# One queue for x and B, one ring of PSUM banks and a new order ahead of the first product, in an S5 scan with a GEGLU feed-forward block

## The chip, the cores and the metric

The kernel runs on one core of a Trainium2 chip. The metric is the device time of one execution in microseconds (us). A profile comes with a *span*, from the first to the last instruction; in the runs shown here the time is about 2 us above the span. A run that is over 1.5% above the fastest of its kernel counts as slow; ratios use fast runs alone. Each run also comes with the mean clock that TensorE was granted, as a share of the full one.

Engines: PE is TensorE (PEld its weight loads), DVE is VectorE, ACT is ScalarE, POOL is GpSimd, SP is SyncE, which here only issues transfers. PSUM is the memory that TensorE's products are written to; the pools below hold eight buffers of it, called banks here.

## The reference, cut to what matters

```python
xn = layernorm(x)                                   # x: 1 x 2048 x 512
# A: diagonal state space model, P = 512 complex states
Bu   = xn @ B_bar.T                                 # B_re, B_im
h[t] = Lam_bar * h[t-1] + Bu[t]
s    = 2 * real(h @ C.T) + xn * Dskip
# B: feed-forward, F = 1376
g    = silu((gelu(xn @ w_gate) * (xn @ w_up)) @ w_down)
out  = x + s * g
```

## The kernel before

The 2048 positions are four stages of 512 (`s`). TensorE's order is u(0), then for each stage: eleven steps (`j`) of gate and up, with the four y products of the stage before laid between them; u of the next stage; the four down products f. VectorE turns u into a real scan by rotating it with cos and sin tables (`pp`, `qq`, `Wt`), scans (`Ft`) and rotates back (`hst`), which y reads. ScalarE evicts u, gate and up from PSUM, that is, copies them out, so that their banks come free. Six "table products" on VectorE build the cos and sin tables first. The order of VectorE's instructions comes from a small model in the kernel with two clocks, `clk["pe"]` and `clk["dve"]`.

```python
ps_mm = ctx.enter_context(tc.tile_pool(name="ps_mm", bufs=4, space=bass.MemoryType.PSUM))  # u, gate, up, B transposes
ps_f  = ctx.enter_context(tc.tile_pool(name="ps_f",  bufs=2, space=bass.MemoryType.PSUM))  # down, warm-up
ps_y  = ctx.enter_context(tc.tile_pool(name="ps_y",  bufs=2, space=bass.MemoryType.PSUM))  # y, x transposes
...
for m in range(M):                                   # x, first stage, SyncE's queue
    nc.sync.dma_start(out=x_tok[:, m, :], in_=x_r[:, m, :])
...
for ri, src in enumerate((A_B_re, A_B_im)):          # B, ScalarE's queue
    nc.scalar.dma_start(out=Bn[:, ri, :, :], in_=...)
...                                                  # then all weights, SyncE's queue
dummies(12)                                          # warm-up products
b_transposes(0)
...
b_transposes(1)                                      # B imaginary, ahead of x on TensorE
dummies(4)
...                                                  # layernorm of x, transposes, copies to xnT
ACT(out=sb[:], in_=ang[:], func=AF.Sin, scale=TWO_PI)
ACT(out=cb[:], in_=kr[:], func=AF.Sin, scale=-TWO_PI, bias=halfpi[:])
nc.vector.tensor_copy(out=sh[:], in_=sb[:])          # fp32 to bf16
nc.vector.tensor_copy(out=ch[:], in_=cb[:])
nc.gpsimd.tensor_copy(out=v4(sa[:]), in_=sh[...])    # widening of the table
...
if s == 0:
    ...
else:
    if j == M: ln_small(s + 1)                       # layernorm of the next stage
    if 6 <= j < 6 + M: ln_out(s + 1, j - 6)          # transposed by SyncE into xnT
    if j in (4, 6, 8, 10): epi(s - 1, m, y_mm(...), ...)
```

## Time and profile before

| | before |
|---|---|
| median of three timed runs | 202.88 us (202.27 to 203.77) |
| the run that was profiled | 201.35 us, span 199.2 us, clock 1.00 |
| first u product starts | 15.03 us |
| B's imaginary half lands | 10.41 us |
| last matmul ends | 195.8 us |

The chain that ended last as shares of the span by engine:

```profile
DVE 47%; PE 30%; ACT 13%; DMA 5%; issue 3%; SPq 0%; ACTq 0%; DVEq 0%
```

TensorE is busy for 93% of the span, yet the chain runs for 47% through VectorE. The two don't contradict each other: while TensorE is busy nearly all the time, many of its waits end on VectorE's work, directly or through ScalarE or a transfer that had waited for it, and the chain then follows VectorE back for many microseconds of unbroken work.

### The profile page before, as it was taken

How to read it: one execution, taken by the hardware profiler on the slowest of the kernel's cores; microseconds unless marked ns; L12 is line 12 of the kernel's file. 1: busy time of each engine (PE TensorE's matmuls, PEld its weight loads, DVE VectorE, ACT ScalarE, POOL GpSimd, SP SyncE). 2: the span in 40 equal slices, each digit the busy share in tenths (PEclk: the TensorE clock that was granted, in tenths of full speed). 3: DMA queues.
4: the chain of work that ended last, by engine and by line, in shares of the span. 5: the costliest groups of instructions: out<-in, count | busy, mean ns of one | idle time of the engine just before them, and what ended most of it. 6: DMA issues, size and time to landing. Idle time of an engine off the chain costs nothing.

```text
span 199.2 us, 2595 instructions
## 1 busy us (share of the span) xinstructions
PE 184.6 (93%) x924; PEld 86.7 (43%) x924; DVE 167.9 (84%) x286; ACT 109.2 (55%) x198; POOL 17.8 (9%) x35
## 2 busy tenths in 40 slices
PE   7478799999999999979999999979989999999993
PEld 2243344444444444444444444434434444454452
DVE  4449999989999779999999889999999999832444
ACT  2434988999327975646425995645423644441210
POOL 3406630000000060000000050000000000000000
PEclk9999999999999999999999999999999999999999
DMA  5999955300000002320000002320000000000001
GB/s 160 357 361 354 174 148 170 79 2 3 0 0 0 0 3 53 79 53 26 0 2 3 0 0 54 81 54 26 0 0 0 3 0 26 26 26 30 26 21 60
DMA packets 21164, 12.26 MB, mean 62 GB/s; under 512 B 11456, under 2 KB 21152, under 8 KB 21152
## 3 DMA queue, kind: packets, MB, share of 16 engines
q1 hardware_dynamic: 20064, 11.05, 21.0%
q10 hardware_dynamic: 1088, 1.05, 1.6%
q8 instruction: 7, 0.11, 0.2%
q14 instruction: 5, 0.04, 0.1%
HBM read 7.38 MB, written 2.10 MB: 48 GB/s over the span
## 4 chain that ended last, share of the span: by engine, by line
DVE 47%; PE 30%; ACT 13%; DMA 5%; issue 3%; SPq 0%; ACTq 0%; DVEq 0%
DVE Ft L389 10%; PE f_ps L445 10%; DVE pp L359 6%; PE y_ps L464 6%; DVE qq L359 6%; PE up_ps L430 6%; PE g_ps L425 6%; ACT junk L519 5%; DMA Bn<-in_A_B_im_dram 4%; ACT ub L437 3%; DVE Wt L363 3%; DVE at L438 3%; ACT gt L435 3%; DVE hst L363 3%; DVE yg L482 2%
## 5 line engine op out<-in xcount | busy, mean ns | idle before, releaser
L425 PE MATMUL g_ps<-xnT,wg 128*128 128x512 bf16 (+1 forms) x176 | 45.2, 379 | 0.0
L430 PE MATMUL up_ps<-xnT,wu 128*128 128x512 bf16 (+1 forms) x176 | 45.2, 379 | 0.0
L445 PE MATMUL f_ps<-wd,at 128*128 128x512 bf16 (+1 forms) x176 | 39.5, 379 | 1.2 <-DVE g L452 1.2
L435 ACT ACTIVATE gt<-g_ps 128x512 bf16<-128x512 f32 (+1 forms) x44 | 26.0, 591 | 16.5 <-PE g_ps L425 16.3
L340 PE MATMUL u_ps<-xnT,BT 128*128 128x512 bf16 x128 | 28.7, 379 | 4.9 <-ACT U L345 2.2
L389 DVE TENSOR_TENSOR_SCAN Ft<-rho,it,Wt 128x512 bf16<-128x512 f32 x24 | 30.3, 1276 | 0.0
L437 ACT ACTIVATE ub<-up_ps 128x512 bf16<-128x512 f32 (+1 forms) x44 | 26.2, 595 | 6.6 <-PE up_ps L430 6.6
L464 PE MATMUL y_ps<-C,hst 128*128 128x512 bf16 x120 | 28.7, 379 | 0.4 <-DVE hst L363 0.3
L450 ACT ACTIVATE th<-f_ps 128x512 f32<-128x512 f32 x16 | 9.6, 597 | 34.3 <-PE f_ps L445 34.3
L445 PEld LDWEIGHTS <-at 128*128 128x128 bf16 (+1 forms) x176 | 17.1, 98 | 22.6 <-issue 2.7
L430 PEld LDWEIGHTS <-wu 128*128 128x128 bf16 (+1 forms) x176 | 17.6, 100 | 20.4
L425 PEld LDWEIGHTS <-wg 128*128 128x128 bf16 (+1 forms) x176 | 17.2, 100 | 18.4
L345 ACT ACTIVATE U<-u_ps 128x512 bf16<-128x512 f32 x32 | 18.2, 598 | 11.4 <-PE u_ps L340 11.3
L438 DVE TENSOR_TENSOR at<-gt,ub 128x512 bf16<-128x512 bf16 (+1 forms) x44 | 18.3, 419 | 6.8 <-ACT ub L437 6.6
L340 PEld LDWEIGHTS <-BT 128*128 128x128 bf16 x128 | 12.4, 98 | 20.0 <-issue 6.0
L464 PEld LDWEIGHTS <-hst 128*128 128x128 bf16 x120 | 11.5, 98 | 14.5 <-DVE hst L363 1.4
L452 DVE SCALAR_TENSOR_TENSOR g<-th,f_ps 128x512 f32<-128x512 f32 x16 | 10.8, 678 | 7.6 <-ACT th L450 7.6
L482 DVE TENSOR_TENSOR yg<-y_ps,g 128x512 bf16<-128x512 f32 x15 | 10.2, 683 | 3.2 <-PE y_ps L469 3.1
L363 DVE TENSOR_TENSOR Wt<-pp,qq 128x1024 bf16<-128x1024 bf16 x16 | 10.8, 688 | 0.2
L363 DVE TENSOR_TENSOR hst<-pp,qq 128x1024 bf16<-128x1024 bf16 x16 | 10.5, 687 | 0.1
L519 ACT ACTIVATE junk<-x_tok 128x512 bf16<-128x512 bf16 x16 | 10.0, 628 | 0.3
L359 DVE TENSOR_TENSOR pp<-U,cos_b 128x2048 bf16<-128x2048 bf16 x8 | 9.8, 1222 | 0.1
(106 smaller groups left out, 157.5 us busy)
## 6 DMA issues: line engine op xcount, KB each, us to landing
out_dram<-ot SPq DMA_DIRECT2D x15, 128.0 KB, 1.7
x_tok<-in_A_x_dram SPq DMA_DIRECT2D x3, 512.0 KB, 3.9
wd<-in_B_w_down_dram SPq DMA_DIRECT2D x1, 1280.0 KB, 10.7
x_tok<-in_A_x_dram SPq DMA_DIRECT2D x4, 128.0 KB, 2.2
Bn<-in_A_B_re_dram ACTq DMA_DIRECT2D x1, 512.0 KB
Bn<-in_A_B_im_dram ACTq DMA_DIRECT2D x1, 512.0 KB, 7.2
wg<-in_B_w_gate_dram SPq DMA_DIRECT2D x1, 512.0 KB, 8.8
wu<-in_B_w_up_dram SPq DMA_DIRECT2D x1, 512.0 KB
```

Source lines behind the costliest of these rows:

```text
L340: nc.tensor.matmul(u_ps[:, :], lhsT=BT[:, ri, kt, pt * P : (pt + 1) * P], rhs=xnT[:, kt, cols], start=(kt == 0), stop=(kt == KT - 1),)
L359: TT(out=box[key][:], in0=src()[:], in1=tab[:, hs, :].unsqueeze(1).to_broadcast(W), op=ALU.mult)
L363: return lambda: TT(out=dst()[i], in0=box["pp"][:, i, :, :], in1=box["qq"][:, 1 - i, :, :], op=op)
L389: nc.vector.tensor_tensor_scan(out=box["F"][:, ri, q, :], data0=rho[:, pt : pt + 1].to_broadcast([P, TS]), data1=box["W"][:, ri, q, :], in ...
L425: nc.tensor.matmul(g_ps[:fs, :], lhsT=wg[:, kt, fsl], rhs=xnT[:, kt, cols], start=(kt == 0), stop=(kt == KT - 1))
L430: nc.tensor.matmul(u_ps[:fs, :], lhsT=wu[:, kt, fsl], rhs=xnT[:, kt, cols], start=(kt == 0), stop=(kt == KT - 1))
L435: ACT(out=gt[:fs], in_=g_ps[:fs, :], func=AF.Gelu_apprx_tanh)
L437: ACT(out=ub[:fs], in_=u_ps[:fs, :], func=AF.Copy)
L438: dve(now() + 0.9, 0.34, lambda: TT(out=at[:fs, j, :], in0=gt[:fs], in1=ub[:fs], op=ALU.mult))
L445: nc.tensor.matmul(f_ps[:, :], lhsT=at[:fs, k, m0 : m0 + P], rhs=wd[:fs, k, :], start=(k == 0), stop=(k == NFT - 1))
L464: nc.tensor.matmul(y_ps[:, :], lhsT=hst[:, j // NPT, j % NPT, m0 : m0 + P], rhs=C2[:, j // NPT, j % NPT, :], start=(j == 0), stop=False,)
L519: ACT(out=junk[:], in_=x_tok[:, s * M + m, :], func=f, accum_out=sx[:, s, i, m : m + 1])
```

## The change

The intent is to start the first product earlier and to let TensorE run on without waiting. The diff, cut to its core:

```diff
-    ps_mm = ... bufs=4 ...   ps_f = ... bufs=2 ...   ps_y = ... bufs=2 ...
+    psum = ctx.enter_context(tc.tile_pool(name="psum", bufs=8, space=bass.MemoryType.PSUM))
     (every PSUM tile: tag="ps" of this pool)
-        nc.scalar.dma_start(out=Bn[:, ri, :, :], in_=src...)
+        nc.sync.dma_start(out=Bn[:, ri, :, :], in_=src...)
-    dummies(12); b_transposes(0); (pt) ; b_transposes(1); dummies(4); (statistics) ... (x transposes)
+    dummies(10); (pt) ; dummies(3); (statistics, norms 0 and 1)
+    b_transposes(0)
+    tps = [t_xn0(0, xs[0]), t_xn0(1, xs[1])]
+    xs += [norm0(2), norm0(3)]
+    b_transposes(1)
+    (xnT copies 0, 1) ; tps += [t_xn0(2, xs[2]), t_xn0(3, xs[3])] ; (xnT copies 2, 3)
-    ACT(out=sb[:], ...Sin); ACT(out=cb[:], ...Sin); nc.vector.tensor_copy(sh, sb); nc.vector.tensor_copy(ch, cb)
+    ACT(out=sh[:], ...Sin); ACT(out=ch[:], ...Sin)
+    (four more Sins of 4 columns in fp32 for c1, s1, cS, sS)
+    Y_AT = (5, 7, 9, 10)
-            (nc.sync).dma_start(out=out_td[...])          # last tile, in halves
+            (nc.sync, nc.scalar)[i].dma_start(out=out_td[...])
-    clk["pe"] = 10.3 ; clk["dve"] = 10.3 ; dve(10.3, 2.8, ln1_stats)
+    clk["pe"] = 9.5  ; clk["dve"] = 11.0 ; dve(11.0, 2.8, ln1_stats)
-                    if j == M: ln_small(s + 1)
-                    if 6 <= j < 6 + M: ln_out(s + 1, j - 6)
-                if j in (4, 6, 8, 10): (y)
+                    if j == M - 1: ln_small(s + 1)
+                    if 5 <= j < 5 + M: ln_out(s + 1, j - 5)
+                if j in Y_AT: (y)
```

## The prediction

> **What bounds the kernel now.** I read the page's busy shares first, then the chain of work that ended last, then the timeline of the first 30 us, then TensorE's own waits. From the page of the kernel before:
>
> ```profile
> span 199.2 us, 2595 instructions
> ...
> PE 184.6 (93%) x924; PEld 86.7 (43%) x924; DVE 167.9 (84%) x286; ACT 109.2 (55%) x198; POOL 17.8 (9%) x35
> ...
> PE   7478799999999999979999999979989999999993
> ```
>
> TensorE is the fullest engine. How much of its 184.6 us is needed? Counted in 512-column products after the first real product: 128 for u, 352 for gate and up, 176 for down, 120 for y, 8 for the last y in halves (16 of 256 columns), 16 for the diagonal (64 of 128 columns): 800. The chain of waits has undisturbed stretches such as "153.39 0.86 PE g_ps L425 x4", 0.216 us a product, so they need 800 x 0.2158 = 172.6 us. The first of them starts at 15.03, the last matmul ends at about 195.8, so the stretch lasts 180.8 us: 8.2 us are lost inside it, 15.0 us lie ahead of it, 3.4 us behind it (last VectorE halves and the output transfer). Everything that can be won is in the 15.0 and the 8.2. The chain of waits (start, length, what) names what holds the 15.0:
>
> ```profile
> 1.18 2.05 DMA x_tok<-in_A_x_dram
> 3.25 7.16 DMA Bn<-in_A_B_im_dram
> 10.46 1.07 PE tb_ps L142 x16
> 11.53 0.86 PE w_ps L135 x4
> 12.65 0.76 DVE xnT L203 x2
> ```
>
> So the second half of B, issued at 3.25, lands only at 10.4; TensorE transposes it in its program order ahead of x, whose first two blocks VectorE had normalised by 8.8. The timeline shows what happens just behind:
>
> ```profile
> 15.03 4.48 PE L340 MATMUL u_ps<-xnT,BT 128*128 128x512 bf16 x20 [0.53 <-DVE xnT L207]
> ...
> 16.57 0.46 ACT L228 ACTIVATE cb<-kr,halfpi 128x196 f32<-128x196 f32 x1
> ...
> 16.90 1.89 POOL L242 COPY sa<-sh 128x2048 bf16<-128x2048 bf16 x1 [0.59 <-DVE sh L229]
> 16.93 0.58 ACT L345 ACTIVATE U<-u_ps 128x512 bf16<-128x512 f32 x1
> 17.06 1.84 DVE L230 CAST ch<-cb 128x196 bf16<-128x196 f32 x1 [0.23 <-ACT cb L228]
> ...
> 18.93 1.91 ACT L328 ACTIVATE ca<-ch 128x2048 bf16<-128x2048 bf16 x1 [1.43 <-DVE ch L230]
> ...
> 20.75 3.15 ACT L345 ACTIVATE U<-u_ps 128x512 bf16<-128x512 f32 x6
> ...
> 21.38 2.75 PE L340 MATMUL u_ps<-xnT,BT 128*128 128x512 bf16 x12 [1.87 <-ACT U L345]
> ```
>
> Read it upwards: TensorE stops because its four banks are full; ScalarE stands behind the ca copy, which waits for a VectorE cast that takes 1.84 us where the same cast of sh took 0.26. Last, TensorE's waits inside the 8.2 us:
>
> ```profile
> PE u_ps L340 <- ACT U L345: 2.2, 2, 1.9
> PE u_ps L340 <- DMA xnT<-xn: 2.2, 2, 1.1
> PE f_ps L445 <- DVE g L452: 1.2, 4, 0.4
> ...
> PE y_ps L464 <- DVE hst L363: 0.3, 1, 0.3
> ```
>
> These are 5.9 us by this view. Measured from start to start of the products around each break (a broken stream also refills) the same places cost about 2.6, 2.5, 2.0 and 0.7 us, 7.8 in all.
>
> **What the Trainium skill says.** (1) "SBUF — State Buffer", section "Who interferes with whom": a cast in a two-port mode and a GpSimd instruction lock each other out for the whole instruction. The trace agrees: the 1.84 us cast runs beside the 1.89 us GpSimd copy and ends just after it. The section also says that a VectorE instruction with at most one SBUF input outside those modes doesn't contend; that would hold for the bn_stats, 0.615 us each. No line here has one beside a GpSimd copy. (2) "DMA: Bandwidth & Descriptors", section "Issuing engines are not separate DMA queues": transfers of several issuers interleave on the same 16 engines. The trace agrees: from 5.5 to 9.5 the weights on SyncE's queue and B on ScalarE's queue share about 355 GB/s. (3) "ScalarE: Activation LUTs", section "What ACT_TABLE_LOAD costs": about 0.19 us plus 0.83 ns an element, 0.09 more for a pointer operand. The 196-column Sin with a bias took 0.46, the one without 0.37, which agrees; four Sins of 4 columns come to 0.2 to 0.3 us each.
>
> **The change part by part.**
>
> *One queue.* x's four issues end at 2.6; B's two now follow at once, and the weights only then. x flows from 1.9 at the issue rate (128 KB each 0.46 us), so its 512 KB are over near 4.2. Then 1 MB of B at the full 350 KB/us seen from 6 us on: real part over at 5.7, imaginary at 7.1, landed about 5.9 and 7.4 against 10.4. The weights lose nothing that counts: total bytes are the same, gate and up are first needed after the u products, and the last of x's second block, whose last packets run near 10.9 now, should be in by 11.
>
> *New order.* VectorE: bn, aggregate as before to 5.0; pf waits for the transpose behind ten warm-up products (5.65); third aggregate and eps end at 6.9; two norms to 7.65; thn, a1; two more norms after GpSimd's power, 8.0 to 8.8. TensorE: B real 6.1 to 7.2, two x transposes to 7.95, B imaginary to 9.0, two x transposes to 9.6. VectorE copies xnT four times at 0.38: 8.8 to 9.55 and, after the last transposes, to about 10.3. ScalarE's four BT evictions at 0.97 end at 10.6, and the last two are not needed by the first product. With 0.3 for a slipping GpSimd power, the first product starts near 10.6: 4.4 us earlier.
>
> *Casts removed.* Sin writes bf16 itself, so 0.26 + 1.84 us leave VectorE, and four small Sins (0.9 us) come to ScalarE. From 10.4: angles 1.45, Sins and small Sins to 13.3, U0, ca to 15.8, then seven evictions at 0.52 to 19.4, table load 1.3. TensorE's u products run 10.6 to 17.5.
>
> *Ring of eight.* With eight banks u writes all its eight tiles unstopped; the gate tile at 17.5 takes the bank of u0, evicted at 13.9; the fifth gate tile at 24.4 takes that of the first gate tile, evicted near 21.4. So the 2.0 us stall goes, and the 0.5 us one near 47. The f tiles take banks of long evicted u tiles: their 2.0 us go.
>
> *Layernorm and y one step earlier or later.* The transposes of xn are issued at steps 5 to 8 rather than 6 to 9, 1.73 us earlier. The two waits for them are about 1.1 each: 2.5 us go. y waits one step more for hst, but VectorE comes late there (below): of 0.7 us, 0.5 stays.
>
> *Output on two queues.* The two last issues don't collide now (0.43 us apart from ot to ot): 0 to 0.2.
>
> Sum: 4.4 + 2.6 + 2.0 + 2.5 + 0.2 = 11.7 less 0.5 for new small waits: 11.2 us. Check from below: 10.6 + 172.6 + 1.4 for waits, refills and pacing + 3.4 = 188.0 us of span, 11.2 under 199.2. Taking 11.2 from the 202.88 median: 191.7 us.
>
> **The rivals.** *VectorE becomes the bound.* From 21.5 to 65 it has hardly a gap, so the hst of the first stage come when its work is done. I followed the kernel's own ordering rule with its new clocks (9.5 and 11.0): at0 now stands behind four table products, not five. VectorE would be there at 19.8, ScalarE gives ub0 only at 21.9, so 2 us of the gain are idle on VectorE. Adding its durations from there puts the last hst at 65.1 (70.96 now), TensorE reaches y at 63.4 and needs the first of that pair at 63.9: a wait of about 0.4, which is why 0.5 stays in my sum. If VectorE is 2 us later than I think, y waits for 2 us: 193.7. In later stages VectorE needs about 35.5 us against TensorE's 43, so it catches up.
>
> *B's transfer is hidden anyway.* If VectorE's chain and not B sets the first product, only the order helps. My lists give 10.3 for VectorE and 9.6 for TensorE, so VectorE takes over as the last step, but 4 us earlier. A slip of the power on GpSimd, or x slower beside nothing, makes it 12: 193.
>
> *The ring couples stages.* A bank comes free only in turn, so a slow VectorE reader of f or y could stop gate tiles eight later. g is read within 2 to 3 us, eight tiles are 5 to 7 us: against it. Only with a late VectorE at the y steps would it cost 1 us.
>
> *SyncE's queue.* The transposes of xn for stage 1 stand behind eight C transposes that issue from 15.6 to 27.4 whatever is done, then 1 MB of x. They then land near 35, and TensorE wants them at 36.6: 1.6 us to spare. Failing that costs 1 us.
>
> **Range and chances.** Floor: nothing lost inside, 10.3 + 172.6 + 3.4 = 186.3 of span, 190.0 of time. Two of the rivals together give 194.8. I take 189.8 to 194.6 round 191.7. Even half of the start's gain and half the waits would be 3%, so faster 0.96, same 0.03, slower 0.01.
>
> **What would show it.** Right: the imaginary half of B lands near 7.4; the first u product starts between 10.2 and 11.2; u's 32 products run as one group; no f_ps and no xnT wait above 0.3 us; no 1.84 us cast. Wrong: a first product after 12, VectorE before at0 idle for over 3 us, y_ps waits of over 1 us, gate tiles that wait for y's reader, or xnT waits in stage 1.

## The result, and the profile after

The changed kernel takes 190.52 us (median of 4, 189.84 to 190.78) against 203.32 (median of 4, 202.27 to 204.12). The ratio is 0.9368, 95% interval 0.9315 to 0.9422. Ratios here are the mean time of one kernel's fast runs over that of the other's of the same rounds, so not quite the ratio of the medians. The span of the profiled runs went from 199.2 to 188.8.

Page of the changed kernel: span, busy time, and the chain by engine.

```profile
span 188.8 us, 2587 instructions
...
PE 181.2 (96%) x918; PEld 85.9 (45%) x918; DVE 165.5 (88%) x284; ACT 108.0 (57%) x202; POOL 21.7 (12%) x35
...
PE 89%; ACT 4%; DMA 2%; DVE 2%; SPq 1%; issue 0%
```

The chain is TensorE's own work for 89% now. What is left to VectorE, ScalarE and DMA lies at the start and in one stretch, from 55 to 65 us.

The chain of waits of the changed kernel at the start (start, length, what):

```profile
2.66 4.57 DMA Bn<-in_A_B_re_dram
...
8.80 1.07 PE tb_ps L140 x16
9.87 0.24 PE tp L171 x4
...
10.94 1.24 PE u_ps L333 x5
```

The first product starts at 10.94 instead of 15.03. The chain still begins with the transfer of B: its real half lets TensorE begin at 7.27 and is the longest piece ahead of the first product; the imaginary half lands at 8.76 (issued at 3.13, 5.6 us to landing in the table of transfers), TensorE transposes it from 8.80 on, and only then come the last two blocks of x.

The timeline of the changed kernel behind the first product:

```profile
10.94 7.07 PE L333 MATMUL u_ps<-xnT,BT 128*128 128x512 bf16 x32 [0.62 <-DVE xnT L212]
...
12.31 1.89 POOL L236 COPY sa<-sh 128x2048 bf16<-128x2048 bf16 x1 [3.94 <-ACT sh L219]
12.54 2.47 DVE L151 BATCH_NORM_STATS2 st<-x_tok 128x6 f32<-128x512 bf16 x4 [0.29 <-DMA x_tok<-in_A_x_dram]
...
15.50 3.50 ACT L338 ACTIVATE U<-u_ps 128x512 bf16<-128x512 f32 x7
...
21.43 0.42 DVE L431 TENSOR_TENSOR at<-gt,ub 128x512 bf16<-128x512 bf16 x1 [1.28 <-ACT ub L430]
```

All 32 u products run as one group, although ScalarE evicts seven of the eight tiles only from 15.50 on: eight banks hold them. The four statistics take 2.47 us beside GpSimd's copy and took 2.46 us alone in the kernel before, so they are not held up as the cast was. The last line shows VectorE idle for 1.28 us ahead of the first `at`, waiting for ScalarE.

TensorE's waits of the changed kernel, all of them (total, times, longest):

```profile
PE tb_ps L140 <- DMA Bn<-in_A_B_re_dram: 1.3, 1, 1.3
PE w_ps L133 <- DVE halfpi L109: 1.2, 1, 1.2
PE y_ps L457 <- DVE hst L356: 1.0, 1, 1.0
PE u_ps L333 <- DVE xnT L212: 0.6, 1, 0.6
```

The waits for `U`, for the transposed `xn` and for `g` are gone. One wait behind the first product remains, of y for `hst`, and it has grown from 0.3 to 1.0. The timeline of VectorE just there:

```profile
62.83 0.43 DVE L431 TENSOR_TENSOR at<-gt,ub 128x512 bf16<-128x512 bf16 x1 [0.78 <-ACT ub L430]
63.17 1.22 DVE L352 TENSOR_TENSOR qq<-Ft,sin_b 128x2048 bf16<-128x2048 bf16 x1
64.42 0.69 DVE L356 TENSOR_TENSOR hst<-pp,qq 128x1024 bf16<-128x1024 bf16 x1
```

`hst` stands behind an `at` in VectorE's order, and that `at` waits 0.78 us for ScalarE. TensorE has begun y at 63.62 and can't go on before 65.17. In the chain of waits the stretch before this, from 55.2 to 62.8, is all ScalarE's: its evictions, and between them six squares of the next stage's layernorm (`junk`, 0.63 us each), which make it late. Moving those was not tried.

### The profile page after: what moved, and what is told of

Read it like the earlier page. It is cut to its first block, busy times and chain, and to the rows that moved or that the text cites. A ratio compares the mean times of both kernels' runs of the same rounds, so it can differ in the third digit from the quotient of the medians.

```text
span 188.8 us, 2587 instructions
## 1 busy us (share of the span) xinstructions
PE 181.2 (96%) x918; PEld 85.9 (45%) x918; DVE 165.5 (88%) x284; ACT 108.0 (57%) x202; POOL 21.7 (12%) x35
## 4 chain that ended last, share of the span: by engine, by line
PE 89%; ACT 4%; DMA 2%; DVE 2%; SPq 1%; issue 0%
PE f_ps L438 20%; PE up_ps L423 18%; PE g_ps L418 18%; PE u_ps L333 15%; PE y_ps L457 14%; DMA Bn<-in_A_B_re_dram 2%; ACT junk L512 2%; PE y_ps L462 2%; PE tb_ps L140 1%; ACT ub L430 1%; PE y_ps L490 1%; SPq L89 1%; ACT gt L428 1%; DVE qq L352 1%; DVE xnT L212 0%; DVE hst L356 0%
## 5 line engine op out<-in xcount | busy, mean ns | idle before, releaser
L438 PE MATMUL f_ps<-wd,at 128*128 128x512 bf16 (+1 forms) x176 | 38.7, 379 | 0.0
L338 ACT ACTIVATE U<-u_ps 128x512 bf16<-128x512 f32 x32 | 17.7, 602 | 8.3 <-PE u_ps L333 8.3
L333 PEld LDWEIGHTS <-BT 128*128 128x128 bf16 x128 | 12.4, 98 | 15.1 <-issue 0.7
L457 PEld LDWEIGHTS <-hst 128*128 128x128 bf16 x120 | 11.5, 98 | 15.1 <-DVE hst L356 2.0
L527 ACT ACTIVATE xn<-x_tok,nb,rs 128x512 bf16<-128x512 bf16 x12 | 9.8, 814 | 6.1 <-POOL nb L523 6.1
L475 DVE TENSOR_TENSOR yg<-y_ps,g 128x512 bf16<-128x512 f32 x15 | 10.3, 684 | 1.9 <-PE y_ps L462 1.8
L356 DVE TENSOR_TENSOR hst<-pp,qq 128x1024 bf16<-128x1024 bf16 x16 | 10.6, 689 | 0.2
L517 POOL TENSOR_SCALAR sx<-sx 128x4 f32<-128x4 f32 x2 | 1.4, 684 | 81.2 <-ACT junk L512 81.2
```

Of the source, the lines that this page charges most:

```text
L333: nc.tensor.matmul(u_ps[:, :], lhsT=BT[:, ri, kt, pt * P : (pt + 1) * P], rhs=xnT[:, kt, cols], start=(kt == 0), stop=(kt == KT - 1),)
L338: ACT(out=U[:, ri, q, :], in_=u_ps[:, :], func=AF.Copy)
L356: return lambda: TT(out=dst()[i], in0=box["pp"][:, i, :, :], in1=box["qq"][:, 1 - i, :, :], op=op)
L438: nc.tensor.matmul(f_ps[:, :], lhsT=at[:fs, k, m0 : m0 + P], rhs=wd[:fs, k, :], start=(k == 0), stop=(k == NFT - 1))
L457: nc.tensor.matmul(y_ps[:, :], lhsT=hst[:, j // NPT, j % NPT, m0 : m0 + P], rhs=C2[:, j // NPT, j % NPT, :], start=(j == 0), stop=False,)
```

## The experiments

"The changed kernel" below is the kernel after the change; its ratio to the kernel before is 0.9368. Each ratio is to the kernel before on the same chip in the same rounds. A difference of two ratios times 203.5 us gives the microseconds quoted as "by the ratios". It compares runs of different rounds, partly on different chips; from the two 95% intervals its uncertainty is estimated at 1.3 to 1.5 us where the run had five rounds (the early and late y, the clocks, the layernorm steps and what follows), and at 1.7 to 2.0 us where it had three. Medians and ranges take in slow runs, ratios don't.

### B back in ScalarE's queue

```diff
-        nc.sync.dma_start(out=Bn[:, ri, :, :], ...)
+        nc.scalar.dma_start(out=Bn[:, ri, :, :], ...)
```

> The changed kernel with B back in ScalarE's queue, beside the weights. If the single queue is what brings B in early: the imaginary half lands near 10.4 instead of 8.76, the first u product starts near 13.2 instead of 10.94, the rest is unmoved: span 191.1, time 192.8 us (1.012 of the changed kernel). If the new order of VectorE alone makes the start and B is hidden anyway: first product below 11.5, time within 0.5 us of 190.5.

Measured: 194.51 us (193.03 to 196.31), ratio 0.9501 (0.9417 to 0.9585), 2.7 us worse by the ratios. The three fast runs have spans of 191.0 to 193.2 against the 191.1 expected. The profiled run fell in the slow state (196.31 us), so its length proves nothing, and how much of what it shows the fast runs share stays open. Its chain, and the two stretches around B's landing (length; busy time of PE, PEld, DVE, ACT and POOL with their instructions; PEclk, the granted clock; the DMA share and GB/s):

```profile
3.42 8.95 DMA Bn<-in_A_B_im_dram
12.42 1.89 PE tb_ps L140 x16
```

```profile
8.50:12.40 3.90, 0.00 (x0) 0.00 (x0) 0.33 (x1) 0.84 (x1) 0.00 (x0) 0.82 1.08 365
12.40:17.70 5.30, 4.76 (x29) 3.28 (x30) 2.82 (x8) 2.99 (x7) 0.65 (x1) 0.50 1.10 363
```

On the shared engines B's imaginary half landed at 12.4 here, 2 us later than in the profile of the kernel before. TensorE idled for 4.2 us, its granted clock fell to 0.50, and the transposes took 1.89 us instead of 1.07. The rival, a time within 0.5 us of 190.5, falls by the fast runs alone, the best of which took 193.03: the new order alone does not make the gain.

### The queue alone

```diff
 (in the kernel before)
-        nc.scalar.dma_start(out=Bn[:, ri, :, :], ...)
+        nc.sync.dma_start(out=Bn[:, ri, :, :], ...)
```

> The kernel before with B behind x in SyncE's queue and nothing else. By the theory B's imaginary half lands near 8.8, the first product starts near 13.4 instead of 15.03 and TensorE's later waits stay (about 7.8 us): time 1.6 us under before, 201.5. By the rival that the queue is the main part of the start's gain: first product near 11, 4 us under before.

Measured: 199.86 us (199.01 to 201.87), ratio 0.9801 (0.9719 to 0.9883); whether that is 2% is unclear by the interval. The profile agrees with the theory: B lands near 9.0, the first product starts at 13.60, and all of TensorE's later waits are as before; the span, 197.8, is 1.4 under that of the profile before. The timed gain, about 4 us by the ratios, is the rival's figure, though the first product is not where the rival had it. The difference seems to be the kernel before's own: its timed runs of these rounds had spans of 200.5 to 203.5 and clocks of 0.972 to 0.991, where its profile had 199.2 and 1.00. The last experiment takes this up.

### Three pools again

```diff
-    psum = ... bufs=8
+    ps_mm = ... bufs=4 ; ps_f = ... bufs=2 ; ps_y = ... bufs=2     (tiles as in the kernel before)
```

> The changed kernel with the three PSUM pools of four, two and two banks as before. If the ring removed the waits on ScalarE's U and on VectorE's g: waits of u, g or up tiles of 1 to 3 us in the first 25 us, 0.5 near 45 and about 2 us before f tiles come back, time 193.5 to 195.5. If the earlier VectorE and ScalarE work has made them disappear by itself: under 1 us, time below 191.5.

Measured: 195.09 us (194.43 to 195.68), ratio 0.9552, 3.7 us worse by the ratios. TensorE's waits:

```profile
PE f_ps L440 <- DVE g L447: 2.0, 2, 1.1
...
PE u_ps L335 <- ACT U L340: 1.0, 2, 0.7
```

The waits return, as the theory had it. One part is smaller: the wait of u in the first stage was 1.9 us before and is 0.7 here, where ScalarE, without the wait for the casts, comes to the remaining u tiles 4.56 us behind the first product instead of 5.72. The ring takes that rest too.

### The casts back

```diff
-    ACT(out=sh[:], ...Sin) ; ACT(out=ch[:], ...Sin) ; (four small Sins)
+    ACT(out=sb[:], ...Sin) ; ACT(out=cb[:], ...Sin)
+    nc.vector.tensor_copy(out=sh[:], in_=sb[:]) ; nc.vector.tensor_copy(out=ch[:], in_=cb[:])
```

> The changed kernel with Sin writing fp32 and VectorE casting to bf16 as before, no small Sins. If the cast's lock with GpSimd cost time: a cast of about 1.8 us is back, ca and the U evictions start 1 us later, VectorE's bn_stats 2.1 us later, and the wait of y for hst grows from 1.3 to 2 to 3 us; with eight banks u itself does not stop: time 191 to 192. If VectorE has slack there (it idles 1.3 us before at): the wait of y grows by under 0.5 us, time within 0.5 us of 190.5.

Measured: 191.08 us (190.66 to 191.83), ratio 0.9369: no difference from 0.9368. The timeline of this kernel shows the slow cast back:

```profile
12.49 1.84 DVE L224 CAST ch<-cb 128x196 bf16<-128x196 f32 x1 [0.23 <-ACT cb L222]
...
22.12 0.42 DVE L433 TENSOR_TENSOR at<-gt,ub 128x512 bf16<-128x512 bf16 x1 [0.26 <-ACT ub L432]
```

VectorE loses 2.1 us to the casts but idles only 0.26 us ahead of `at` instead of 1.28; the rest is ScalarE's, which gives `at` its input 1.0 us later, counted from the first product. y's wait stays 0.9. With a ring of eight banks, removing the 1.84 us cast is worth nothing measurable: half of what VectorE saved, it spent waiting.

### y one step earlier, and later

```diff
-    Y_AT = (5, 7, 9, 10)
+    Y_AT = (4, 6, 8, 10)
```

> The changed kernel with y at steps 4, 6, 8, 10 as before. If the step of y sets its wait for hst: the y wait grows from 1.3 to between 2 and 3 us because hst comes at the same time and y asks 1.7 us earlier: span 189.8 to 190.5, time 191.5 to 192.2. If VectorE's order moves with it (hst is pulled ahead of at tiles when y asks): the wait stays below 1.8 us, time within 0.5 of 190.5.

Measured: 193.84 us (192.42 to 194.59), ratio 0.9498, 2.6 us worse. More than expected. The timeline of TensorE, and the stretch just behind the wait (columns as above):

```profile
65.39 2.64 PE L457 MATMUL y_ps<-C,hst 128*128 128x512 bf16 x6 [2.67 <-DVE hst L356]
```

```profile
65.20:69.00 3.80, 3.62 (x12) 1.59 (x13) 1.67 (x4) 0.14 (x1) 2.55 (x6) 0.55 0.00 0
```

The wait is 2.67 us, and behind it the clock is 0.55 for 3.8 us: six products take 2.64 us instead of the 1.68 us that six take in the changed kernel. By the trace's clock records it is 0.50 for 3.41 us, from 65.53 on. Five of the six runs have a mean clock of 0.99, which such a stretch would give (estimated: 1 - 0.5 x 3.41 / 192 = 0.991); one has 0.999 and the shortest span. So a wait of this length can be paid twice, but need not be: in the profile of the kernel before, the wait of 2.50 us for B was followed by the full clock.

```diff
-    Y_AT = (5, 7, 9, 10)
+    Y_AT = (6, 8, 9, 10)
```

> The changed kernel with y at steps 6, 8, 9, 10. If y is merely too early for VectorE: the wait of 1.3 us falls below 0.3, no other appears, span 187.6, time 189.3. If y's readers then hold up the banks of later tiles or hst moves later too: another wait of 1 us, time as 190.5 or above.

Measured: 190.49 us (190.28 to 192.66), ratio 0.9365: no gain. The wait of y is gone and two others are there:

```profile
PE up_ps L423 <- DVE g L445: 1.9, 2, 1.4
...
PE u_ps L333 <- DVE yg L475: 1.0, 1, 1.0
```

An up tile waits for the reader of an f tile, a u tile for the reader of a y tile. In the ring a bank comes free in turn only, so a VectorE reader that is late for f or y stops a product that has nothing to do with it. The changed kernel's profile has no such wait; one step of y is enough to bring them. This profile is of one of the two longer runs, though (spans of 190.1 and 190.7; the other four have 188.2 to 188.6), so most runs may wait less.

### The ordering clocks of before

```diff
-    clk["pe"] = 9.5  ; clk["dve"] = 11.0 ; dve(11.0, 2.8, ln1_stats)
+    clk["pe"] = 10.3 ; clk["dve"] = 10.3 ; dve(10.3, 2.8, ln1_stats)
```

> The changed kernel with the clocks that order VectorE's work set back to 10.3 and 10.3, which puts at0 behind five table products instead of four. If VectorE's 1.28 us of idleness before at0 is what makes hst late for y: the idle time goes below 0.2, hst comes 1.1 us earlier, the y wait falls from 1.3 to below 0.4, span 187.8, time 189.5. If the lost time is made up or lost elsewhere before y: the y wait stays above 1, time 190.5.

Measured: 189.21 us (188.78 to 190.06), ratio 0.9276 (0.9239 to 0.9313), 1.9 us better than the changed kernel by the ratios. All of TensorE's waits:

```profile
PE w_ps L133 <- DVE halfpi L109: 1.2, 1, 1.2
PE u_ps L333 <- DVE xnT L212: 0.6, 1, 0.6
PE tb_ps L140 <- DMA Bn<-in_A_B_re_dram: 0.2, 1, 0.2
```

On VectorE a fifth table product, of 1.25 us from 20.05 on, fills the idle time before the first `at`, and no wait behind the first product is left. The edit moves many instructions of VectorE, so the idle time is not all that it changes; also `hst` no longer stands behind the late `at`. But the wait of y, 1.3 us with its refill, is what the run wins in the profile beside the 0.6 us earlier start of this run; the two make up nearly all of the 2.0 us between the spans, 188.8 and 186.8.

### The layernorm steps of before, alone and with the early y

```diff
-                    if j == M - 1: ... if 5 <= j < 5 + M: ln_out(s + 1, j - 5)
+                    if j == M: ...     if 6 <= j < 6 + M: ln_out(s + 1, j - 6)
```

> The changed kernel with the layernorm steps back at 6 to 9. If the earlier steps removed the two waits for the transposed xn (1.2 and 1.3 us): they come back with 1 us each, time 192.5. If the later y steps 9 and 10 give the transposes room anyway (TensorE has 1.9 us more work behind step 9): no such wait above 0.3 us, time within 0.4 of 190.5; and ScalarE's wait of 4.0 us for GpSimd's nb shrinks.

Measured: 190.56 us (190.29 to 191.15), ratio 0.9341 (0.9302 to 0.9379). No wait for the transposed `xn` comes back. So the earlier layernorm step, to which the prediction gave 2.5 us, is not needed for them. Both old steps together:

> The changed kernel with both the layernorm steps (6 to 9) and the y steps (4, 6, 8, 10) as before. Either alone left no wait for the transposed xn. If each of the two is enough by itself: both undone bring back two waits of about 1.2 us each, on top of the 2.8 us wait of y seen with the early y: time 2.0 to 2.5 us above that run, 196. If it is the ring or the start that removed the xnT waits: none above 0.3 us, time as with the early y alone, 193.8.

Measured: 195.31 us (193.88 to 197.35), ratio 0.9585, against 0.9498 with the early y alone: 1.8 us more. Beside the same wait of y, 2.7, the table of waits has:

```profile
PE u_ps L333 <- DMA xnT<-xn: 1.6, 3, 1.1
```

The waits return when both are undone. Either the earlier layernorm or the later y (two y products behind step 9 rather than one) suffices; the change does the same thing twice.

### x ahead of B's imaginary half on TensorE

In the kernels with the changed start, the first product follows B's landing. Landing of the imaginary half and start of the first product, in us, from eight profiles: 8.76 and 10.94 (the changed kernel), 8.31 and 10.49 (three pools), 8.98 and 11.17 (y early), 7.85 and 10.23 (y late), 8.47 and 10.66 (casts), 8.14 and 10.33 (old clocks), 9.11 and 11.29 (layernorm), 8.25 and 10.43 (both steps). The difference is 2.18 or 2.19 in seven of them, 2.38 where B lands earliest. This does not single out the imaginary half: the first product also starts 3.47 to 3.67 behind the start of TensorE's work on the real half, and in all eight TensorE comes to the imaginary half less than 0.2 us before it can start on it. In the seven, TensorE's wait ahead of that work ends with the real half's landing. In the eighth (y late) no such wait is left, because its warm-up products last until 6.93.

```diff
-    b_transposes(1)
     (xnT copies 0, 1) ; tps += [t_xn0(2, xs[2]), t_xn0(3, xs[3])]
+    b_transposes(1)
 ...
-        for q in range(H2):          (u tiles: real, imaginary, real, imaginary)
-            for ri in range(2):
+        for ri in range(2):          (real, real, imaginary, imaginary)
+            for q in range(H2):
```

> The changed kernel with TensorE's last two transposes of x ahead of those of B's imaginary half, and the u products of a half ordered real, real, imaginary, imaginary. In eight traces the first product starts 2.18 us behind the landing of B's imaginary half, except where that lands before 8 us. If B's landing sets the start: the first product now starts near 10.0, no longer tied to that landing, and the span falls by 0.5 to 1.0 us to about 188.0, time 189.7. If VectorE's chain sets it, as the prediction had it: first product at 10.3 or later when B lands early, no gain (190.5). If ScalarE's late eviction of the imaginary BT takes its place: a wait of 0.5 to 1 us at the third u tile and no gain.

Measured: 190.49 us (190.15 to 190.70), ratio 0.9369: no gain in time. The first product does start earlier, at 9.99 with B landed at 8.11, where the rule above gives 10.29; in the run below B landed at 7.79 and the first product started at 9.99 too, so it no longer follows B. VectorE sets it now: in both runs it makes its four copies to `xnT` without a pause from 8.53 on, and the last ends at 9.94 or 9.95. A line of TensorE's waits shows where it went, beside y's wait of 0.9 as ever:

```profile
PE u_ps L333 <- DMA xnT<-xn: 0.3, 1, 0.3
```

It is new, and it is in the first stage: TensorE comes to u(1) at 35.9 and starts it at 36.39. SyncE issues the four transposes of `xn` only after eight of C and 1 MB of x, from 29.79 on, and the one issued at 32.50 lands at 35.87, the last after it. The timed spans, 188.1 to 188.7, equal those of the changed kernel, 187.9 to 188.9.

With the clocks of before added:

```diff
+    (as above)
-    clk["pe"] = 9.5  ; clk["dve"] = 11.0 ; dve(11.0, 2.8, ln1_stats)
+    clk["pe"] = 10.3 ; clk["dve"] = 10.3 ; dve(10.3, 2.8, ln1_stats)
```

> The order of the previous but one run (x transposes first, real products first) and the ordering clocks of 10.3 and 10.3 together. With the y wait gone (186.8 us of span with those clocks alone) only the start is left to win: span 186.0 to 186.5, time 188.4 to 188.9. If the earlier start only makes VectorE later for y: y wait of 0.5 us, time 189.2.

Measured: 188.76 us (188.37 to 190.35), ratio 0.9294 (0.9250 to 0.9338), with 0.9276 for the clocks alone: the same. Its start is 0.34 us earlier than with the clocks alone, and at u(1), 36.10 against 36.22, a third of that is left. Both versions beat the changed kernel and the kernel before, by some 1% and 7%; the simpler edit, the clocks alone, is the one to keep.

### The kernel before, kept warm

```diff
 (in the kernel before)
+    dummies(10)
     b_transposes(1)
     dummies(4)
```

> The kernel before with ten more warm-up products, 2.2 us, in TensorE's wait for B's imaginary half. The timed runs of the kernel before have mean clocks of 0.972 to 0.992 and spans of 200.3 to 203.5, the profiled one 1.0 and 199.2. If the idle wait lets the clock fall and the first products then run at half speed: clocks of 0.995 and more, spans of 199.5 to 201.5, time 0.5 to 2 us below before. If the low clock comes from elsewhere or only the landing itself varies: clocks as of before, time within 0.4 us of before.

Measured: 201.92 us (200.92 to 204.26) against 203.52 in these rounds, ratio 0.9912 (0.9861 to 0.9964): the interval lies below 1. Five of the six runs have clocks of 0.997 to 1.00; the sixth, at 0.992, is slow. Ten of the kernel before's eleven runs have 0.983 to 0.992. So doing more useless work while B is awaited makes the kernel 1.8 us faster: the idle wait costs clock. A clock of 0.992 or 0.983 would be one or two stretches like the 3.41 us at half clock seen with the early y (an estimate). That they lie on the first products is not seen in the kernel before, whose one profile has the full clock; the slow profile with B in ScalarE's queue shows such a case. B's landing varies beside that; in the chain of this profile

```profile
3.45 8.09 DMA Bn<-in_A_B_im_dram
11.59 1.07 PE tb_ps L142 x16
```

it is 11.5, 1.1 us later than in the profile before.

## Why the prediction was right, and where its steps were not

Predicted 191.7, measured 190.52, inside the range; of its signs of being right one failed, B's landing near 7.4. Term by term, in the profiled spans, from start to start of the products around each break:

| step | predicted | measured |
|---|---|---|
| first product earlier | 4.4 | 15.03 - 10.94 = 4.1 |
| waits of u for ScalarE | 2.6 | 2.6 |
| waits of f for VectorE | 2.0 | 2.0 |
| waits for the transposed xn | 2.5 | 2.5 |
| wait of y for hst | +0.2 | 0.7 before, 1.3 after: -0.6 |
| output on two queues | 0 to 0.2 | tail 3.4 before, 3.5 after: -0.1 |
| new small waits | -0.5 | none |
| sum | 11.2 | 10.5 (the spans differ by 10.4) |

*The start.* The size was right, the reason given for it was not. The prediction had B landing at 7.4 and VectorE setting the first product, at 10.3 to 10.6. B landed at 8.8. In part, x and B did not move at the "full 350 KB/us" so early: the changed kernel moves 149, 256, 176 and 261 GB/s in the four microseconds from 1.5 on. But by 7.5 it has moved some 1.58 MB, as much as x and B together; in the packets of the trace the first weights start at 6.95 and the last of B at 8.41, so weights overtook the rest of B. B's landing therefore still sets the start in seven of eight profiles, and in the eighth the warm-up products do. VectorE's copies come last there, but they wait for TensorE's transposes: 0.78 us in the changed kernel, about 0.1 where B lands earliest. VectorE's own chain sets the start only with x ahead of B's imaginary half, and at 9.99 rather than 10.3. The prediction's own sum for x was also loose: four issues of 0.46 from 1.9 on end at 3.7, not 4.2. "B's transfer is hidden anyway" was listed as a rival and "VectorE takes over" was the answer given; the runs say B.

*The queue and the order.* The queue alone won 1.4 us in the profile and some 4 us in time; taken out of the changed kernel it costs 2.7. In the profiles the first product starts at 13.60 with the queue alone, at 15.68 with the order alone (a slow run) and at 10.94 with both.

*The ring.* Right in mechanism and size: the waits go with it and come back without it. The coupling that it brings was called a rival of 1 us "only with a late VectorE at the y steps". The changed kernel shows none; with y one step later it shows 1.9 and 1.0 us.

*The casts.* The prediction gave no time to them by themselves but counted their removal into the chain that ended the wait of u. Putting them back into the changed kernel costs nothing. The reason was in the prediction's own rival: VectorE would be early for `at0` and idle 2 us. It idled 1.28.

*Layernorm a step earlier.* The 2.5 us are there, the attribution is half of the truth: the later y gives the same by itself.

*y.* The wait of about 0.4 (0.5 in the sum) was mis-sized: it is 1.0, or 1.3 with the refill. The sum of VectorE's durations left out that the `at` in front of `qq` would wait 0.78 us for ScalarE, although the trace of the kernel before has the same gap.

*Output and SyncE's queue.* The two output queues show no gain in the tail; they were not tried alone. The transposes of xn for stage 1 were to land near 35: the third of the four lands at 36.02, and TensorE starts u(1) at 36.84, so less was to spare than the 1.6 us of the prediction. With the earlier start this rival cost 0.3.

*From the span to the time.* The prediction took its 11.2 us from the median of 202.88, which lies 3.7 above the profiled span. After the change that distance is 1.7. The kernel before's profile was one of its best executions, 201.35; its timed ones lose more. The warm-up experiment recovers 1.8 us of that, so a clock that falls while TensorE waits for B is a good part; later landings may be another. So the prediction was 0.8 too hopeful in the span and 2.0 too cautious in this step; the two errors left 1.2 us, and it was partly luck that they had opposite signs. The floor of 190.0 rests on the same 3.7 and was wrong: with the clocks of before the median is 189.21, with the shortest spans at 186.8, above the floor of the span, 186.3.

What stays open: why transfers run below their later rate in the first four microseconds, and why B's two halves land where they do; and whether SyncE's queue, with the transposes of xn ahead of the later x blocks, would let the earlier start count.

## What to carry to other kernels

Take the distance between the profiled execution and the timed median as something to explain before predicting: here a good part of it was a wait that lets the clock fall, and the change shortened it. When a wait on an engine goes, look at what that engine does next: half of the two microseconds saved on VectorE became idle time, until the order of its instructions was changed to use them. And one ring for all tiles is worth its banks as long as every reader is quick; a late reader of one kind of tile then stops products of another.

## What the Trainium skill lacked or had wrong

- "TensorE: Matmul & The Clock Gate", section "HAM oscillation — how this bites in real kernels", gives as its abstract rule "no PE-idle gaps >~3.4µs." Here shorter gaps were enough, though not each time: after waits of 2.67 us (y early) and 2.68 us (both old steps) the traces' clock records show 3.41 us at half clock, while a wait of 2.50 us in the kernel before was followed by the full clock. Of these two kernels' twelve runs, three have a mean clock of 0.999 or 1.00.
- "DMA: Bandwidth & Descriptors", section "Issuing engines are not separate DMA queues", says that transfers of several issuers interleave and that issuing from several engines saves only the sequencer's time. It doesn't say what the interleaving costs a transfer that is needed first: 512 KB issued at about 3.1 to 3.5 on a queue of its own, beside weights on another, landed at 10.4, 11.5 and 12.4 in three profiles; on the one queue ahead of the weights between 7.8 and 9.1 in eleven.
- No page gives the rate of transfers in the first microseconds of a kernel. Here they ran at 149, 256, 176 and 261 GB/s in the four microseconds from 1.5 on, and at 331 to 381 in the six after. The cause is not known.
